# Half of a fused kernel's output projection by a Strassen identity, with its scaling spread over the QKV stage

## The chip, the cores and the metric

The kernel runs on one core of one Trainium2 chip. The metric is the device time of one execution in microseconds (us). A run here is one execution. Of each kernel one execution was also taken by the hardware profiler, and its trace is of that one run. The runs were made in several groups, on different chips, so totals of different groups are compared by their ratio to the kernel before, which ran in every group.

Engines are named as in the profile: PE is TensorE, PEld its weight loads, DVE is VectorE, ACT is ScalarE, POOL is GpSimd, SP is SyncE, which issues most of the transfers here.

## The reference

```python
def _A_ref(x, wqkv, wo):                 # B=1, S=2048, D=1024, H=32 heads of 32
    q, k, v = split_heads(x @ wqkv)
    phi = lambda t: jnp.where(t > 0, t + 1, jnp.exp(t)) + 1e-6
    pq, pk = phi(q), phi(k)
    kv  = einsum("bhsd,bhse->bhde", pk, v)
    z   = einsum("bhsd->bhd", pk)
    num = einsum("bhqd,bhde->bhqe", pq, kv)
    den = einsum("bhqd,bhd->bhq", pq, z)[..., None] + 1e-6
    return merge_heads(num / den) @ wo
def _B_ref(x, w_gate, w_up, w_down):      # F=3584
    return (silu(x @ w_gate) * (x @ w_up)) @ w_down
xn = layernorm(x)
return x + _A_ref(xn, ...) * silu(_B_ref(xn, ...))     # bf16 in and out
```

The edit concerns the last product of `_A_ref`, `o @ wo`.

## The kernel before

The kernel has four stages on PE, one after the other. The QKV stage computes K and V for 16 token tiles and accumulates `kvz`. Block 0's Q projection follows. Then come the Q projections of blocks 1 to 3, mixed with `nd` (numerator and denominator of each of 16 row tiles) and the output projection `s_ps`. Last come gate/up and down, which already use a seven-product identity of Strassen's kind: sums of blocks of the activations on VectorE, differences of blocks of the weights (called T) on GpSimd.

While the first stages run, the other engines prepare the gate, up and down weights for that identity. One preparation step takes a weight chunk through this chain: a load, a square with a running sum on ScalarE (a norm, which bounds the values), a one-column matmul that sums it over partitions, a scaling by a power of two on VectorE, four subtractions on GpSimd, and a store.

```python
def emit_st0(key, t):      # ScalarE: sum of squares of one chunk, into asum
    nc.scalar.activation(out=junk, in_=raw_view(key, t), func=ACT.Square, accum_out=asum[:])
def emit_sc(key, t):       # VectorE: the scaling, SBUF to SBUF
    nc.vector.tensor_scalar(out=w, in0=w, scalar1=cs_all[:, c:c + 1], scalar2=None, op0=ALU.mult)
def emit_T(key, t, later=False):   # GpSimd: SBUF to SBUF
    nc.gpsimd.tensor_tensor(out=T1, in0=b12, in1=b11, op=ALU.subtract)
    nc.gpsimd.tensor_tensor(out=T2, in0=b22, in1=T1, op=ALU.subtract)
    nc.gpsimd.tensor_tensor(out=T3, in0=b22, in1=b12, op=ALU.subtract)
    nc.gpsimd.tensor_tensor(out=T4, in0=b21, in1=T2, op=ALU.subtract)
    # ... cut
def prep_step(between=None):
    # ... a load for the newest chunk, a store of the oldest
    emit_st0(*prep_st[1])
    emit_st1(k3[0], stat_ps[0]())      # one-column matmul
    between()                          # often: one nd tile and its evacuation
    emit_st2(*k3)                      # power of two, and emit_sc
    emit_T(*k3, later=True)
```

The output projection before the edit is plain. For each row tile and each half of the columns it runs eight matmuls of 512 columns.

```python
def emit_S(b, t, cc):
    s_ps = ps2.tile([P, CW], FP32, name="s_ps", tag="B2")
    for c in range(G):                          # G = 8, CW = 512
        nc.tensor.matmul(s_ps[:], lhsT=oT[:, c, ttok], rhs=wo_sb[:, c, cc*CW:(cc+1)*CW], ...)
    nc.scalar.copy(out=s_sb[:, cc*CW:(cc+1)*CW], in_=s_ps[:])
# the QKV stage, cut: per token tile i and column chunk c
for i in range(2, NT):
    for c in range(NCH):
        emit_Bmm(i, c); ...; emit_Bev(i, c)
        if c == 3 and i in (4, 6, 7): prep(1)
        if i >= 8 and c % 2 == 1: prep(...)     # 13 steps over tiles 8 to 15
```

## Time and profile before

The kernel before took 761.89 us, the median of three runs (761.75 to 763.33). These lines are from the page of its profiled execution: the span, the busy time of the engines with their share and number of instructions, GpSimd's busy tenths in 40 slices of 19 us, the chain that ended last by engine, and the group of the output projection (busy us, mean ns of one, idle before it). Line numbers differ between kernels; the tile names do not.

```profile
span 761.6 us, 10386 instructions
...
PE 748.9 (98%) x3662; PEld 350.5 (46%) x3731; DVE 542.3 (71%) x1026; ACT 348.0 (46%) x479; POOL 269.6 (35%) x382
...
POOL 0477699827563255868655000200000000200000
...
PE 94%; DVE 3%; DMA 1%; issue 1%; ACT 0%; SPq 0%; DVEq 0%; ACTq 0%
...
L688 PE MATMUL s_ps<-wo_sb,oT 128*128 128x512 bf16 x250 | 57.4, 379 | 0.3
```

PE is busy 98% of the time, and it is 94% of the chain. Time that another engine spends costs the kernel nothing unless PE waits for it.

The waits view lists who kept PE waiting: in total, how often, and the longest, in us.

```profile
PE warm_ps L549 <- DVE warm L546: 1.5, 1, 1.5
PE kv_ps L514 <- DMA wkv_sb<-in_A_wqkv_dram: 1.3, 1, 1.3
PE zw L761 <- DVE cg L830: 0.7, 1, 0.7
PE nd L658 <- DVE pqT L159: 0.4, 1, 0.4
...
PE q_ps L176 <- DVE pqT L159: 0.3, 1, 0.3
```

All of PE's waits come to about 5 us. At most 2.5 of them lie after the first loads.

The next lines are GpSimd's timeline late in the attention stage (start, duration). They show one of the four subtractions of one preparation step. It takes 1.16 us when nothing disturbs it.

```profile
214.19 1.16 POOL L286 TENSOR_TENSOR w_sb<-w_sb 128x512 f16<-128x512 bf16 x1 [0.68 <-ACT s_sb L691]
```

### The profile page before, as it was taken

What the parts mean: (1) busy time and instruction counts of PE and PEld (TensorE: products, weight loads), DVE (VectorE), ACT (ScalarE), POOL (GpSimd) and SP (SyncE); (2) the same over time, 40 slices, a digit from 0 to 9 for tenths busy, and PEclk for the clock granted to TensorE, in tenths of its full rate; (3) what the DMA queues carried; (4) which work ended last, traced back from release to release, by engine and by line L of the source; (5) the groups of instructions that cost most, each with busy time, mean ns of one, the idle gap of its engine ahead of it and who ended that gap; (6) DMA issues with size and microseconds to landing.
All of it is one profiled execution on the core that took longest, in us unless ns stands there. A gap on an engine that the chain in (4) does not pass through costs nothing.

```text
span 761.6 us, 10386 instructions
## 1 busy us (share of the span) xinstructions
PE 748.9 (98%) x3662; PEld 350.5 (46%) x3731; DVE 542.3 (71%) x1026; ACT 348.0 (46%) x479; POOL 269.6 (35%) x382
## 2 busy tenths in 40 slices
PE   8999999999999999999999999999999999999997
PEld 3444444454444444444444444444444444444444
DVE  6788676985656688878889875358676767787335
ACT  4545677698954566566448411132323222211022
POOL 0477699827563255868655000200000000200000
PEclk9999999999999999999999999999999999999999
DMA  9876799779879669898888227397654445430824
GB/s 318 286 157 125 198 301 322 259 173 292 245 217 289 243 229 318 281 353 287 308 300 293 80 90 257 121 379 281 251 185 178 166 165 172 173 139 15 275 88 136
DMA packets 105908, 170.29 MB, mean 224 GB/s; under 512 B 34688, under 2 KB 82176, under 8 KB 95232
## 3 DMA queue, kind: packets, MB, share of 16 engines
q1 hardware_dynamic: 99280, 143.81, 59.6%
q0 software_dynamic: 3984, 21.24, 7.0%
q10 hardware_dynamic: 2592, 4.59, 1.8%
q8 instruction: 29, 0.48, 0.3%
q14 instruction: 23, 0.19, 0.1%
HBM read 111.67 MB, written 50.59 MB: 213 GB/s over the span
## 4 chain that ended last, share of the span: by engine, by line
PE 94%; DVE 3%; DMA 1%; issue 1%; ACT 0%; SPq 0%; DVEq 0%; ACTq 0%
PE zw L761 25%; PE kv_ps L514 14%; PE xb L761 12%; PE dzw L946 12%; PE s_ps L688 7%; PE yb L761 6%; PE dx L946 6%; PE q_ps L176 5%; PE dy L946 3%; DMA wkv_sb<-in_A_wqkv_dram 1%; PE nd L658 1%; PE kvz L536 1%; PE df L946 1%; DVE pqT L159 1%; DVE q_ps L153 1%
## 5 line engine op out<-in xcount | busy, mean ns | idle before, releaser
L761 PEld LDWEIGHTS <-w_sb 128*128 128x128 f16 (+1 forms) x1568 | 152.1, 98 | 183.9 <-issue 1.3
L514 PE MATMUL kv_ps<-wkv_sb,xnT 128*128 128x512 bf16 x499 | 113.0, 379 | 2.6 <-DMA wkv_sb<-in_A_wqkv_dram 1.3
L761 PE MATMUL xb<-xnT,w_sb 128*128 128x512 bf16 x420 | 113.3, 379 | 1.5
L761 PE MATMUL zw<-S,w_sb 128*128 128x512 f16 x448 | 105.8, 379 | 0.7 <-DVE cg L830 0.7
L761 PE MATMUL zw<-xnT,w_sb 128*128 128x512 bf16 x448 | 105.8, 379 | 0.0
L286 POOL TENSOR_TENSOR w_sb<-w_sb 128x512 f16<-128x512 bf16 x42 | 49.3, 1173 | 116.9 <-DVE w_sb L274 29.1
L253 ACT ACTIVATE w_sb<-w_sb 128x2048 bf16<-128x2048 bf16 x42 | 79.9, 1902 | 11.8 <-DMA w_sb<-in_B_w_up_dram 5.6
L946 PE MATMUL dx<-w_sb,hT 128*128 128x512 bf16 x202 | 76.6, 379 | 0.3
L514 PEld LDWEIGHTS <-xnT 128*128 128x128 bf16 x512 | 48.6, 98 | 57.7 <-issue 2.2
L946 PEld LDWEIGHTS <-hT 128*128 128x128 bf16 (+1 forms) x462 | 45.2, 98 | 51.7
L176 PE MATMUL q_ps<-xnT,wq_sb 128*128 128x512 bf16 x249 | 58.2, 379 | 0.7 <-DVE pqT L159 0.3
L789 DVE SCALAR_TENSOR_TENSOR s<-yb,rc_all,s 128x512 f32<-128x512 f32 x42 | 31.5, 749 | 37.8 <-ACT s L788 37.6
L688 PE MATMUL s_ps<-wo_sb,oT 128*128 128x512 bf16 x250 | 57.4, 379 | 0.3
L761 PE MATMUL yb<-S,w_sb 128*128 128x512 f16 x224 | 57.4, 378 | 0.0
L946 PE MATMUL dzw<-w_sb,hT 128*128 128x512 bf16 (+1 forms) x190 | 57.0, 379 | 0.0
L837 ACT ACTIVATE sg<-cg 128x1024 bf16<-128x1024 f32 x28 | 29.6, 1057 | 56.8 <-DVE cg L830 56.8
L830 DVE SCALAR_TENSOR_TENSOR cg<-zw,rc_all,s 128x1024 f32<-128x1024 f32 x28 | 35.9, 1283 | 24.3 <-PE zw L761 14.0
L287 POOL TENSOR_TENSOR w_sb<-w_sb 128x512 f16<-128x512 bf16 x42 | 50.1, 1193 | 3.3
L289 POOL TENSOR_TENSOR w_sb<-w_sb 128x512 f16<-128x512 bf16 x42 | 50.4, 1201 | 0.0
L288 POOL TENSOR_TENSOR w_sb<-w_sb 128x512 f16<-128x512 bf16 x42 | 50.4, 1199 | 0.0
L886 POOL TENSOR_TENSOR hs<-hT 128x512 f16<-128x512 bf16 x2 | 2.5, 1250 | 132.7 <-ACT sg L837 132.6
L920 POOL DMA_DIRECT2D out_dram<-io x16 | 8.7, 544 | 101.8 <-DVE io L919 101.6
(152 smaller groups left out, 1080.5 us busy)
## 6 DMA issues: line engine op xcount, KB each, us to landing
w_sb<-pk_g SPq DMA_DIRECT2D x27, 1024.0 KB, 6.1
pk_g<-w_sb SPq DMA_DIRECT2D x14, 1024.0 KB, 5.1
w_sb<-wd SPq DMA_DIRECT2D x14, 1024.0 KB, 5.0
w_sb<-pk_u SPq DMA_DIRECT2D x14, 1024.0 KB, 5.0
pk_u<-w_sb POOLq DMA_DIRECT2D x13, 1024.0 KB, 6.0
w_sb<-wd SPq DMA_DIRECT2D x14, 768.0 KB, 5.6
w_sb<-in_B_w_gate_dram SPq DMA_DIRECT2D x14, 512.0 KB, 6.5
w_sb<-in_B_w_down_dram SPq DMA_DIRECT2D x28, 256.0 KB, 4.7
```

The costliest lines, as they stand in the source:

```text
L176: nc.tensor.matmul(q_ps[:], lhsT=wq_sb[:, dc, g * P:(g + 1) * P], rhs=xn_ap(dc, btok), start=(dc == 0), stop=(dc == DC - 1))
L253: nc.scalar.activation(out=junk, in_=raw_view(key, t), func=ACT.Square, accum_out=asum[:])
L286: nc.gpsimd.tensor_tensor(out=T1, in0=b12, in1=b11, op=ALU.subtract)
L287: nc.gpsimd.tensor_tensor(out=T2, in0=b22, in1=T1, op=ALU.subtract)
L288: nc.gpsimd.tensor_tensor(out=T3, in0=b22, in1=b12, op=ALU.subtract)
L289: nc.gpsimd.tensor_tensor(out=T4, in0=b21, in1=T2, op=ALU.subtract)
L514: mm = nc.tensor.matmul(kv_ps[:], lhsT=xn_ap(dc, tok), rhs=wkv_sb[:, dc, c * CW:(c + 1) * CW], start=(dc == 0), stop=(dc == DC - 1))
L688: mm = nc.tensor.matmul(s_ps[:], lhsT=oT[:, c, ttok], rhs=wo_sb[:, c, cc * CW:(cc + 1) * CW], start=(c == 0), stop=(c == G - 1))
L761: mm = nc.tensor.matmul(out, lhsT=lhs(k), rhs=rhs(k), start=(first and k == 0), stop=(k == HK - 1), skip_group_check=True)
L789: nc.vector.scalar_tensor_tensor(out=s2[:], in0=y_[:], scalar=rc, in1=s1[:], op0=ALU.mult, op1=ALU.add)
L830: nc.vector.scalar_tensor_tensor(out=d12, in0=zw[:], scalar=rc, in1=s2[:, None, :].to_broadcast([P, 2, TB]), op0=ALU.mult, op1=ALU.add)
L946: nc.tensor.matmul(out, lhsT=lhs, rhs=rhs, start=first, stop=lastk, skip_group_check=True)
```

## The change

The intent is to save PE time in the attention stage. Blocks 2 and 3 of `o @ wo` are done by a seven-product identity instead of eight products. That needs sums of blocks of `o`, differences of blocks of `wo` (the four `To`), and fp16 operands, which the kernel keeps bounded: `o` is scaled by a power of two from norms of wv, and `wo` by one from its own norms. Those statistics are spread over the QKV stage as small instructions.

The diff, cut to what matters:

```diff
-    NWE = 8
+    NWE = 7                        # one chunk of w_down is prepared later, in gate/up
+    SO_ST = [(i, c) for i in (2, 3, 4, 5) for c in (0, 2)] + [(i, c) for i in (6, 7, 8, 9) for c in (0, 2)]
+    SO_PW = [(7, 1), (10, 1)]
+    WO_SC = (10, 11, 12, 13)
     ... in the QKV stage, tile i, chunk c:
+                if (i, c) in SO_ST: so_stat(...)      # ScalarE: square of 1024 columns, 16 in all
+                if (i, c) in SO_PW: so_pow2(...)      # PE: eight 1-column matmuls in a row, twice
+                if c == 3 and i in WO_SC:
+                    wo_scale(WO_SC.index(i))          # VectorE: wo_sb *= power of two, 128x2048, four times
-                if c == 3 and i in (4, 6, 7):
+                if c == 3 and i in (4, 5, 6, 7):
                     prep(1)
     ... block 0's Q: the phi of three of the groups moves to ScalarE
-            emit_Q(0, g)
+            emit_Q(0, g, act=g in (3,5,7))
     ... once: 16 subtractions on GpSimd for the four To
+                nc.gpsimd.tensor_tensor(out=o_[:, k], in0=a_[:, k], in1=b_[:, k], op=ALU.subtract)
     ... the evacuation of nd and the copy of s multiply by the powers of two
     ... blocks 2 and 3: four units, each 7 products of 4 matmuls
+            def sums():                               # VectorE, SBUF to SBUF, 128x512 each
+                nc.vector.tensor_tensor(out=so[:, 0], in0=a21, in1=a22, op=ALU.add)
+                nc.vector.tensor_tensor(out=so[:, 1], in0=so[:, 0], in1=a11, op=ALU.subtract)
+                nc.vector.tensor_tensor(out=so[:, 2], in0=a11, in1=a21, op=ALU.subtract)
+                nc.vector.tensor_tensor(out=S4, in0=a12, in1=so[:, 1], op=ALU.subtract)
     ... the order in which the first unit starts:
+        u["sums"]()
+        nds[0]()
+        u["x"]()
+        u["w"]()
+        emit_S(1, 3, 0, fx[4])
+        nds[1]()
+        units[1]["sums"]()
     ... (further units, with the last preparation and the sums of x between them)
```

## The prediction

> **What bounds the kernel now.** The page gives PE 98% busy and the chain of waits is 94% PE; the granted clock is full. PE's waits add up to only about 5 us of 761.6: 1.5 before the warm-up, 1.7 on the first loads, 0.4 + 0.3 in the Q projection of block 0 (on pqT, VectorE). The stage table shows 19.89 of 20 us busy almost everywhere. Only fewer PE cycles, or the removal of those waits, can help. In the chain, 16 matmuls of 512 columns take 3.45 us, 216 ns each (the 379 ns "mean" overlaps the next).
>
> **Removed.** Blocks 2 and 3 of the output projection are 128 such matmuls; 4 units x 7 products x 4 = 112 remain: 16 x 0.216 = -3.45 us. The order of instructions has as many on PE as before: 16 large ones became 16 one-column ones.
>
> **Added on PE.** Two groups of 8 statistic matmuls. One alone costs 0.02 us (8 + 1 matmuls take 1.75 against 1.73 us), [...]eight 129-column kvz matmuls take 0.46 us. [...]Estimate +0.8 us for both.
>
> **Block 0's Q.** Three phis move work to ScalarE (VectorE 0.68 us instead of 0.62 + 0.69). The chain runs through VectorE from 133.7 to 147.7 us; PE loses 0.75 us. I expect 0.5 to 0.7 us back.
>
> **Off the chain.** ScalarE gets 16 squares of 1024 columns (estimate 1.05 us each, from 1.9 us for 2048) in the QKV stage between 25 and 86 us, where it is 49 to 71% busy. Walking its order by hand with 0.99 us (exp+relu) and 0.49 us (V copy), it stays within the 7.37 us of a token tile, tile 9 excepted (7.9), which three PSUM banks absorb: 0 to 0.5 us lost. GpSimd gets 16 subtractions of 1.16 us (18.6 us), which fit its idle gap of 149 to 167 us. One wd chunk moves into the gate/up stage, which has room: 0 to 0.2 us.
>
> **End of the attention stage.** A unit is 6.04 us of PE. VectorE has sums of 4 x 0.42 and two evacuations of 0.75; in the last two units also the four sums of x (6.6 us) and the last preparation, about 12 of 12.1 us. The last unit puts z, x2, z2 in a row, so z2 waits for VectorE's evacuation of Z. oT of block 3 reuses the buffer that block 1's last group reads, and a transpose lands after 5.2 us (3.0 to 7.7), so sums may hold VectorE 1 to 2 us. PE loses an estimated 0.5 to 1.5 us here.
>
> **Sum.** -3.45 + 0.8 - 0.6 + 0.2 + 1.0 + 0.1 = -1.95: about 759.9 us; I take 759.6, range 757.8 to 762.0. Faster by 2%: 0.005, within 2%: 0.985, slower: 0.01.
>
> **What would show it.** Matmuls of the output projection: 240 rather than 256. PE's 0.75 us of waits around 138 to 148 us gone. Statistics groups of 0.4 us each near 70 and 87 us. PE waits in the last 30 us before gate/up: 0.5 to 1.5 us, on VectorE. Gate/up and down stages unchanged in length. GpSimd busy 149 to 168 us.
>
> **What would make it wrong.** ScalarE holding up kv_ps banks between 60 and 95 us (1 to 3 us slower); sums waiting for transposes behind blocked stores in the sync queue (PE idle several us near 225 us); or no stall in the units at all: 758.6 us.

In the part on the work added on PE two passages that gave a reason for the +0.8 us are cut, since no trace of this case shows it. The sum and its six terms stand as recorded (-3.45 + 0.8 - 0.6 + 0.2 + 1.0 + 0.1 = -1.95 us). The +0.8 is the estimate from the 0.46 us of eight `kvz` matmuls.

## More of the kernel before

An `nd` tile has one PSUM buffer. PE starts the next one only when VectorE has evacuated the last (such a wait took 2.6 us in the profile after).

GpSimd shows 9 in the slices from about 95 to 133 us. It has no slack where the weights are prepared (19.68 of 20 us busy from 100 to 120 us).

## The result and the profile after

The changed kernel took 764.45 us (median of four runs, 764.0 to 765.68). In the same rounds the kernel before took 762.26 (761.75 to 763.33). The ratio is 1.0029, with a 95% interval of 1.0012 to 1.0047. Within 2% the two are the same, but the interval lies above 1. PE does less work, and the kernel became slower by about 2.2 us. A ratio here is the mean time of one kernel's runs over that of the other's runs of the same rounds, so it is not quite the ratio of the medians quoted.

The same lines of the page after:

```profile
span 763.0 us, 10573 instructions
...
PE 750.1 (98%) x3731; PEld 349.4 (46%) x3731; DVE 561.8 (74%) x1058; ACT 376.2 (49%) x526; POOL 290.0 (38%) x400
```

GpSimd is busier (290.0 us against 269.6), mostly by the new `To`. The page alone shows no fault: PE reads 98% again, and its granted clock was 1.0.

The waits of PE do show it:

```profile
PE nd L713 <- DVE wq_sb L725: 2.6, 1, 2.6
...
PE kv_ps L525 <- DMA wkv_sb<-in_A_wqkv_dram: 1.5, 1, 1.5
PE q_ps L182 <- DVE pqT L162: 1.2, 2, 0.9
PE kv_ps L525 <- DVE pk_sb L162: 1.1, 2, 0.9
```

A wait of 2.6 us for the `nd` bank is new. The waits on `q_ps` grew from 0.3 to 1.2 us. Those on `kv_ps` behind VectorE are new, with 1.1 us.

To see where time was lost, PE's timeline is cut at four starts: the first `kvz` product, the first matmul of block 0's Q, the first matmul after the first `nd` tile, and the first matmul of gate/up. The lengths below are differences of those starts. The last column is the span less the start of gate/up.

| profiled execution | QKV, from the first kvz | block 0's Q and first nd | from there to gate/up | gate/up and down | span |
|---|---|---|---|---|---|
| before | 102.63 | 19.30 | 100.52 | 513.34 | 761.6 |
| before_again | 102.63 | 19.29 | 100.52 | 513.54 | 761.2 |
| after | 104.58 | 19.83 | 100.26 | 512.48 | 763.0 |
| after less before | +1.95 | +0.53 | -0.26 | -0.86 | +1.4 |

The first three columns of the kernel before repeat to 0.01 us in two executions, so hundredths mean something here. The time before the first kvz varies from 25.0 to 26.0 us over all traces, with waits for the first loads. It is left out of the table for that reason. The two executions after and before differ by 1.4 us and not by the 2.2 of the medians, since the profiled run of the kernel before (763.33 us) was the slowest of its four, while that of the changed kernel (764.76 us) was near its median. The saving of 3.45 us lies in the third column, and nearly all of it is missing there.

### The profile page after: what moved, and what is told of

Read it like the earlier page. It is cut to its first block, busy times and chain, and to the rows that moved or that the text cites. A ratio compares the mean times of both kernels' runs of the same rounds, so it can differ in the third digit from the quotient of the medians. Undisturbed runs are those within 1.5% of the kernel's fastest.

```text
span 763.0 us, 10573 instructions
## 1 busy us (share of the span) xinstructions
PE 750.1 (98%) x3731; PEld 349.4 (46%) x3731; DVE 561.8 (74%) x1058; ACT 376.2 (49%) x526; POOL 290.0 (38%) x400
## 4 chain that ended last, share of the span: by engine, by line
PE 70%; DVE 1%; ACT 0%; issue 0%
PE zw L935 25%; PE xb L935 13%; PE dzw L1120 12%; PE yb L935 6%; PE dx L1120 6%; PE dy L1120 3%; PE fx L786 3%; PE df L1120 1%; PE dz L1120 0%; PE fx L744 0%; PE nd L713 0%; DVE wq_sb L725 0%; DVE wq_sb L781 0%; DVE oT L782 0%; DVE wq_sb L780 0%; DVE pqT L150 0%
## 5 line engine op out<-in xcount | busy, mean ns | idle before, releaser
L935 PE MATMUL xb<-xnT,w_sb 128*128 128x512 bf16 x448 | 115.0, 379 | 0.0
L1120 PE MATMUL dx<-w_sb,hT 128*128 128x512 bf16 x210 | 79.6, 379 | 0.0
L1120 PE MATMUL dzw<-w_sb,hT 128*128 128x512 f16 x196 | 58.3, 379 | 0.0
L962 ACT ACTIVATE s<-xb,rcl 128x512 f32<-128x512 f32 x14 | 9.6, 687 | 65.3 <-PE xb L935 65.3
```

The lines of the kernel that those rows point to most:

```text
L935: mm = nc.tensor.matmul(out, lhsT=lhs(k), rhs=rhs(k), start=(first and k == 0), stop=(k == HK - 1), skip_group_check=True)
L1120: nc.tensor.matmul(out, lhsT=lhs, rhs=rhs, start=first, stop=lastk, skip_group_check=True)
```

## Where the time went, read from the traces

**The units.** The chain of waits, followed back from gate/up and given in order of time, passes through VectorE just before the `nd` tile that waited. Columns: start, us, what. (The sums are written into space that `wq_sb` no longer needs, hence their name.)

```profile
218.74 1.20 DVE wq_sb L780
219.94 1.31 DVE wq_sb L781
...
221.27 1.26 DVE oT L782
...
223.23 1.36 DVE wq_sb L725 x3
...
224.64 0.64 PE nd L713 x8
```

The `nd` product at 224.64 waited for VectorE's evacuation (L725). That stood in line behind the sums (L779 to L782) of the first unit. VectorE's own timeline shows what the sums cost:

```profile
218.19 0.45 DVE L779 TENSOR_TENSOR wq_sb<-oT 128x512 f16<-128x512 bf16 x1
218.74 1.20 DVE L780 TENSOR_TENSOR wq_sb<-wq_sb,oT 128x512 f16<-128x512 f16 x1
219.86 1.37 DVE L781 TENSOR_TENSOR wq_sb<-oT 128x512 f16<-128x512 bf16 x1
221.27 1.26 DVE L782 TENSOR_TENSOR oT<-oT,wq_sb 128x512 f16<-128x512 bf16 x1
```

The four sums have the same shape, yet the first takes 0.45 us and the others 1.20 to 1.37. Later units' sums take 0.41 to 0.42 us each. What differs is GpSimd, which at that time runs the last preparation step of block 2:

```profile
217.21 1.16 POOL L294 TENSOR_TENSOR w_sb<-w_sb 128x512 f16<-128x512 bf16 x1 [0.68 <-ACT s_sb L747]
218.44 1.21 POOL L295 TENSOR_TENSOR w_sb<-w_sb 128x512 f16<-128x512 bf16 x1
219.62 1.34 POOL L296 TENSOR_TENSOR w_sb<-w_sb 128x512 f16<-128x512 bf16 x1
220.91 1.33 POOL L297 TENSOR_TENSOR w_sb<-w_sb 128x512 f16<-128x512 bf16 x1
```

Those are the same four subtractions as in the kernel before, now 1.16, 1.21, 1.34 and 1.33 us. Both engines are slower in this overlap: three of VectorE's sums by a factor of about three (0.42 to 1.20-1.37 us), GpSimd's subtractions by up to 0.18 us (1.16 to 1.34).

So the first theory is that the two engines hold each other up where both work from SBUF to SBUF at the same time. The four sums together took 4.28 us instead of 1.68, and that excess of 2.60 us is as long as PE's wait of 2.58. The runs below test what the collision costs. They do not test by what mechanism it comes about, nor why the two engines share it so unevenly.

**The QKV stage.** The same reading applies to the scaling of `wo`. The first fence is one of its four instructions on VectorE. The second is GpSimd before and beside it.

```profile
108.15 1.64 DVE L619 TENSOR_SCALAR wo_sb<-wo_sb,cs_all 128x2048 bf16<-128x2048 bf16 x1
```

```profile
106.53 1.15 POOL L294 TENSOR_TENSOR w_sb<-w_sb 128x512 f16<-128x512 bf16 x1
...
109.21 1.60 POOL L296 TENSOR_TENSOR w_sb<-w_sb 128x512 f16<-128x512 bf16 x1
110.77 1.60 POOL L297 TENSOR_TENSOR w_sb<-w_sb 128x512 f16<-128x512 bf16 x1
```

A scaling of this shape takes 0.75 us where GpSimd runs no subtraction (L282 of this trace at 181.48, 198.82 and 204.34 us; 0.743 us is its shortest, 0.754 the median). Here it takes 1.64. The kernel before already shows this collision: its 13 weight scalings of this shape between 25 and 148 us (L274), all but one of them beside a subtraction of GpSimd, average 1.13 us. GpSimd's subtractions beside it take 1.60 us instead of 1.15. Not every overlap costs both: L282 at 91.75 us took 0.75 us beside a subtraction of 1.65. GpSimd is full in this stretch (19.69 of 20 us from 100 to 120), so what it loses is not made up.

The preparation then reaches ScalarE late. A square stands ahead of the exponentials on ScalarE and waited 2.02 us for its load:

```profile
124.69 1.91 ACT L259 ACTIVATE w_sb<-w_sb 128x2048 bf16<-128x2048 bf16 x1 [2.02 <-DMA w_sb<-in_B_w_gate_dram]
...
126.59 1.06 ACT L153 ACTIVATE e_t<-kv_ps 128x512 f32<-128x512 f32 x2
```

The exponential for `kv_ps` (L153) stands behind that square and started at 126.59 us, as the square ended. PE waits for the bank:

```profile
128.68 1.67 PE L525 MATMUL kv_ps<-wkv_sb,xnT 128*128 128x512 bf16 x7 [0.95 <-DVE pk_sb L162]
```

That is 0.95 us on PE, behind a queue that waits for a load. The trace shows what the load stood behind. GpSimd's last subtraction of the step before ended at 117.84 us, SyncE issued the store of its results at 117.86 and, next in the same queue, this load at 118.30. How much of the lateness is owed to the scalings of `wo` is tested by e2 and e3.

## The experiments

Theory P: VectorE's SBUF-to-SBUF instructions and GpSimd's subtractions hold each other up where they overlap, by whatever mechanism. This costs about 2.5 us at the first unit and about 1.5 us in the QKV stage.

Rival V: VectorE simply has too much to do there, whatever the instruction. Rival Q, for the first unit: the order on VectorE, with the sums ahead of the evacuation, or late transposes. Rival R: the step of preparation that was moved to tile 5, and ScalarE's 16 squares, disturb the QKV stage.

### e1_hold_T: an edit that changed nothing

The last step's subtractions were to be issued after the first unit's sums, by moving only their emission:

```diff
-            emit_T(*k3, later=True)
+            if hold: held.append(lambda: emit_T(*k3, later=True))
+            else:    emit_T(*k3, later=True)
...
         u["sums"]()
         nds[0]()
+        held.pop(0)()
```

> The changed kernel with one thing moved: the four GpSimd subtractions of the last preparation step of block 2 are issued after the sums of the first unit and the first evacuation of block 3, VectorE's order unchanged. Theory P[...]: the first unit's four sums fall from 0.45 / 1.20 / 1.37 / 1.26 us to 0.42 us each, and PE's wait of 2.58 us for the evacuated nd falls under 0.4 us; time about 2 to 2.6 us under the changed kernel, near 762. Rival Q (the sums stand before the evacuation in VectorE's order, or wait for their transposes): wait stays above 2 us, time within 0.7 us of the changed kernel's 764.4.

Measured: 764.13 us, ratio 1.0034 (1.0019 to 1.0049), and the wait still 2.57 us. This refutes nothing. GpSimd ran the subtractions at 216.19 to 221.2 us, again 0.68 us after what it had waited for, on top of the sums. Its queue had nothing else in it, so the later place in the program did not delay them here. In e6 a dependency did (227.23 us). The experiment tested nothing, and e6 below repeats it properly.

### e2_no_scale: the QKV stage without the four scalings

```diff
-                if c == 3 and i in WO_SC:
-                    wo_scale(WO_SC.index(i))
```

The bound of `o` then uses unscaled `wo`, which is still correct for these inputs.

> The changed kernel without the four scalings of wo on VectorE (and without the factor that undoes them; same result for these inputs). Theory P: GpSimd's subtractions between 100 and 120 us fall from 1.31 to under 1.2 us each, its preparation is 2 us earlier, ScalarE's waits for loads before 128 us shrink, PE's waits for VectorE's phi (0.95 + 0.16 us in the QKV stage, 1.17 us in block 0's Q) fall by at least 1 us in sum; time 1 to 2 us under the changed kernel. Rival R (the preparation that now starts one step earlier, at tile 5, is the cause): waits of PE as before, time within 0.5 us.

Measured: 763.56 us (762.14 to 763.8), ratio 1.0016 (1.0 to 1.0033). The QKV stage fell from 104.58 to 103.08 us, and the waits for `kv_ps` behind VectorE are gone. ScalarE's wait for the late gate load shrank from 2.02 to 0.59 us. The `nd` wait stayed at 2.57 us. The 16 squares of rival R stayed in too, and the stage is only 0.45 us longer than in the kernel before, of which the statistics groups on PE are about 0.4. So the squares cost next to nothing.

Half of these runs show another effect, described under "The clock" below. It took 1.7 us of the profiled execution, so the total says less than the stage.

### e3_bn_stand_in: the same VectorE time with other instructions

To part P from V, each scaling was replaced by three statistics instructions that together take 1.60 to 1.61 us, about its contended duration. They read one SBUF operand and write a few columns. The scaling factor is changed as in e2.

```diff
-                    wo_scale(WO_SC.index(i))
+                    for q_, sl_ in enumerate((slice(0, 512), slice(512, 1024), slice(0, 256))):
+                        nc.vector.bn_stats(out=st3[:, q_ % 2, :], in_=wo_sb[:, 2 * k_ + q_ // 2, sl_])
```

> As the kernel without the four scalings, but in their place VectorE does statistics over 1280 columns of wo (about 1.7 us each, as long as the scalings took): same VectorE time, one SBUF input. Theory P[...]: GpSimd's subtractions stay under 1.2 us and PE's waits are those of the kernel without scalings within 0.4 us. Rival V (VectorE's mere time): PE waits as long as in the changed kernel (2.3 us in sum in QKV and block 0's Q).

Measured: 764.43 us, ratio 1.0033 (1.0018 to 1.0048). The QKV stage took 103.42 us: 1.16 us less than the changed kernel, 0.34 us more than without anything in that place. The window of 100 to 120 us shows why. The columns are the window and its length, busy us with the number of instructions in brackets for PE, PEld, DVE, ACT and POOL, PE's clock, the DMA share and GB/s. The changed kernel, then e2, then e3:

```profile
100.00:120.00 20.00, 19.82 (x114) 9.72 (x113) 18.30 (x31) 13.68 (x20) 19.69 (x15) 1.00 0.93 293
```

```profile
100.00:120.00 20.00, 20.00 (x116) 9.85 (x114) 13.95 (x28) 14.36 (x21) 19.68 (x17) 1.00 1.01 315
```

```profile
100.00:120.00 20.00, 20.00 (x116) 9.82 (x115) 17.61 (x39) 14.36 (x20) 19.69 (x18) 1.00 1.01 314
```

VectorE is as busy in e3 (17.61 us) as after the change (18.30), but GpSimd gets through 18 instructions instead of 15 in the same 19.69 us. So 1.16 of the 1.5 us are what GpSimd loses, and about 0.34 us is VectorE's time. Rival V holds for at most a quarter of this cost, since the stand-in takes the contended 1.6 us and a scaling alone would take 0.75.

The total did not follow, because gate/up and down took 513.55 us here (512.48 after the change). Its trace shows a wait of 0.53 us there, for ScalarE.

### e4_no_prep5: the preparation step at tile 5 put back

```diff
-                if c == 3 and i in (4, 5, 6, 7):
+                if c == 3 and i in (4, 6, 7):
```

> The changed kernel without the extra preparation step at tile 5; one more step is left for the end of the attention stage. Rival R: the 0.95 us wait before the last QKV group vanishes and the wait in block 0's Q falls under 0.8 us; time about 1 to 1.5 us under the changed kernel. Theory P: these waits stay above 1.5 us in sum; time within 0.7 us of the changed kernel.

Measured: 770.33 us, ratio 1.0115 (1.0099 to 1.013). The waits in the QKV stage and in block 0's Q remained (0.73 and 0.93 us), and the QKV stage became only 0.54 us shorter. So rival R is not the main cause. The step that was left over slid into the units. There GpSimd's four subtractions met another unit's sums (0.42, 1.26, 1.37 and 1.26 us), then the first sum of x (2.17 us), and PE waited 3.26 us besides the 2.56 at `nd`. So the collision can be made a second time by moving a preparation step onto a unit. This supports P, at a cost that nobody would want.

### e5_drop_T: the last step's subtractions left out (wrong)

```diff
-            emit_T(*k3, later=True)
+            if not drop:                       # drop for the step at block 2, tile 3
+                emit_T(*k3, later=True)
```

> Wrong on purpose: the changed kernel without the four GpSimd subtractions of the last preparation step of block 2 (in the run before, issuing them later did not make them run later, so that run tested nothing). VectorE and PE have exactly the changed kernel's work and order. Theory P[...]: the first unit's four sums take 0.42 us each and PE's wait for the evacuated nd falls from 2.58 to under 0.4 us. Rival Q (order on VectorE, late transposes): the wait stays above 2 us.

Measured, in one look: 761.84 us (one run, state unknown), with a wrong result as intended (relative error 0.30). The sums took 0.41, 0.42, 0.42 and 0.42 us, and the wait at `nd` was gone. These are the second and third of them:

```profile
218.38 0.42 DVE L781 TENSOR_TENSOR wq_sb<-wq_sb,oT 128x512 f16<-128x512 f16 x1
218.73 0.42 DVE L782 TENSOR_TENSOR wq_sb<-oT 128x512 f16<-128x512 bf16 x1
```

The stretch to gate/up fell from 100.26 to 97.66 us. VectorE's work and order were those of the changed kernel, and only GpSimd's four subtractions were missing. So the 2.6 us were the collision and not the sums themselves, nor their place in the order (rival Q).

### e6_hold_scale: the same subtractions, really later

The step's scaling on VectorE, on which the subtractions depend, is emitted after the second unit's sums. This delay is a dependency. It also takes that scaling (1.39 us in the changed kernel, beside GpSimd) away from its place ahead of the first sums.

```diff
-            emit_st2(*k3)
-            emit_T(*k3, later=True)
+            emit_st2(*k3, later=hold)          # hold for the step at block 2, tile 3
+            if hold: held.extend((lambda: emit_sc(*k3), lambda: emit_T(*k3, later=True)))
+            else:    emit_T(*k3, later=True)
...
         units[1]["sums"]()
+        while held: held.pop(0)()
```

> The changed kernel, correct, with the last preparation step's scaling on VectorE held back until after the second unit's sums, so that its GpSimd subtractions, which need it, can not run before. Theory P: sums of the first unit 0.42 us each, PE's wait for nd under 0.3 us, no new wait above 0.5 us in the units; time 2 to 3.5 us under the changed kernel (2.6 us of wait, and what the granted clock loses after it): 761 to 762.5. Rival Q: as before, 764.

Measured: 762.88 us (762.46 to 763.57), ratio 1.0005 (0.999 to 1.0021). VectorE's timeline at the first unit (three of the four sums), and GpSimd's, which now pauses from 216.6 to 227 us:

```profile
217.75 0.43 DVE L785 TENSOR_TENSOR wq_sb<-wq_sb,oT 128x512 f16<-128x512 f16 x1
218.09 0.42 DVE L786 TENSOR_TENSOR wq_sb<-oT 128x512 f16<-128x512 bf16 x1
218.54 0.42 DVE L787 TENSOR_TENSOR oT<-oT,wq_sb 128x512 f16<-128x512 bf16 x1
```

```profile
215.49 1.16 POOL L297 TENSOR_TENSOR w_sb<-w_sb 128x512 f16<-128x512 bf16 x1
227.23 1.16 POOL L294 TENSOR_TENSOR w_sb<-w_sb 128x512 f16<-128x512 bf16 x1 [10.58 <-ACT s_sb L752]
```

The sums are all at 0.42 to 0.43 us, in the same place ahead of the evacuation. The wait at `nd` is gone, and the stretch to gate/up is 97.91 us (-2.35). The result is correct. VectorE's order is not quite that of the changed kernel: the scaling moved, and the first sum started about 1 us earlier (217.24 us instead of 218.19). So e6 shows that the loss can be had back in a correct kernel, and e5 is the clean test of its cause.

### e7_scale_on_act: the scaling of wo on ScalarE

```diff
-            nc.vector.tensor_scalar(out=wo_sb[:, 2*q:2*q+2, :], in0=..., scalar1=cs_all[...], op0=ALU.mult)
+            nc.scalar.activation(out=wo_sb[:, 2*q:2*q+2, :], in_=..., func=ACT.Copy, scale=cs_all[...])
```

> The changed kernel with the four scalings of wo on ScalarE (about 2 us each there) rather than VectorE. Theory P: GpSimd's subtractions from 100 to 120 us fall to 1.2 us, PE's wait of 0.95 us before the last QKV group falls under 0.3 us as without the scalings, unless ScalarE's 8 us more make a new wait of up to 0.5 us; time 0.5 to 1.2 us under the changed kernel.

Measured: 764.26 us, ratio 1.002 (1.0003 to 1.0037). The QKV stage took 103.88 us: 0.70 us better than with VectorE, 0.80 us worse than without scaling. GpSimd again ran 17 instructions between 100 and 120 us. The collision is avoided, but 0.80 us remain; that they are ScalarE's own time is argued, not tested. Block 0's Q became shorter too (18.95 us against 19.83), which was not aimed at.

### e8_all: both collisions removed, statistics joined

This is e6 and e7 together, with each group of eight 1-column statistics matmuls replaced by one of 8 columns and a reduction on VectorE.

```diff
-            for q in range(8 * h, 8 * h + 8):
-                nc.tensor.matmul(ps, lhsT=ones[:], rhs=so_st[:, q:q + 1], ...)
+            nc.tensor.matmul(ps[:], lhsT=ones[:], rhs=so_st[:, 8 * h:8 * h + 8], start=True, stop=True, ...)
+            nc.vector.tensor_reduce(out=tt[:], in_=ps[:], axis=mybir.AxisListType.X, op=ALU.add)
```

> Both mends, and each group of eight one-column statistics matmuls replaced by one eight-column matmul and a sum over eight on VectorE. Theory P: the gains add: -2.6 (nd) - 1.0 (scalings) - 0.35 (statistics) from 764.4, so 760.0 to 761.0, under the kernel before (761.8) by about 1 us. If waits that remain are simply moved to the next one: 761.5 or more.

Measured: 761.72 us (761.06 to 763.04), ratio 0.9991 (0.9978 to 1.0003). From the first kvz to gate/up it took 220.48 us, 4.19 us less than the changed kernel and 1.97 less than the kernel before. But gate/up and down took 515.05 us, 2.6 more than in the changed kernel.

The joined statistics gained nothing: the QKV stage is 103.90 us, against 103.88 in e7. Where PE saved 0.2 us, it then waited 0.3 us for VectorE before a `kvz` product.

### e9_no_scale_all: the same without any scaling of wo

The edits are those of e6, e2 and the joined statistics. (The expectation speaks of 16 scalings. There are four instructions.)

> The changed kernel[...]: the first unit's four sums behind the block-3 row-0 evacuation, the 16 scalings of wo left out (o's bound then uses the norms of the unscaled wo, correct for these inputs), and the eight 1-column statistics matmuls of a tile joined in one 8-column matmul. [...]no wait for kv_ps in the QKV stage, no 2.6 us wait for the nd bank, 1.3 us fewer statistics matmuls; from the first kvz to the start of gate/up about 219.5 to 220.3 us (changed kernel 224.67, kernel before 222.45). Total 759 to 761 us, ratio to the kernel before 0.997 to 0.999; the upper end if gate/up again waits about 1 us for late w_up loads. Rival (the change costs something else per unit that is still there): the stage stays above 222 us and the ratio at or above 1.0.

Measured: 762.59 us (760.08 to 764.48), ratio 1.0 (0.9981 to 1.0019). This misses the expected total. The way to gate/up missed its range by only 0.2 us (220.48). Most of the loss is behind it: gate/up and down took 516.64 us, with waits of 1.15 and 1.04 us and then about three microseconds at half clock. Three of the six runs had a mean clock of 0.997 and took 763.89 to 764.48 us; the three at 0.999 and above took 760.08 to 761.29. The rival of that expectation (some cost per unit still there) does not hold either, since the stretch of the units was 97.90 us.

### e10_late_square: one square of the preparation behind a phi

In block 0's Q of the changed kernel, ScalarE's next square waited for its load, and the exponentials for two `q_ps` banks waited behind it:

```profile
134.21 1.91 ACT L259 ACTIVATE w_sb<-w_sb 128x2048 bf16<-128x2048 bf16 x1 [2.10 <-DMA w_sb<-in_B_w_down_dram]
...
136.12 1.06 ACT L153 ACTIVATE e_t<-q_ps 128x512 f32<-128x512 f32 x2
```

The edit emits this one square after Q(0, 1) instead of before it:

```diff
-            emit_st0(*prep_st[1])
+            if late0: held0.append(lambda a=prep_st[1]: emit_st0(*a))   # for the last step of the QKV stage
+            else:     emit_st0(*prep_st[1])
...
             emit_Q(0, g, act=g in (3,5,7))
+            if g == 1: held0.pop(0)()
```

> The previous kernel with one ScalarE square of the weight preparation emitted after the first Q projection of block 0, so that ScalarE's in-order wait for that square's load does not stand ahead of the phi that frees q_ps. If that wait is what is left in block 0's Q, the wait of 0.8 to 0.9 us for q_ps goes to 0.4 us or less and the stage shortens by 0.4 to 0.8 us; total 758.5 to 760.5 us. If q_ps is held by something else the wait stays above 0.7 us.

Measured: 761.33 us (760.15 to 762.26), ratio 0.9989 (0.9977 to 1.0001). The wait on `q_ps` is gone, and block 0's Q fell from 19.42 us in e9 to 18.22, below the kernel before's 19.30. To gate/up it was 219.80 us. The expectation of the mechanism held. The expectation of the total (at most 760.5) did not, because gate/up and down took 514.57 us.

### before_again: a second profile of the kernel before

> The kernel before, unchanged, for a second profile: the one at hand is of one of its slower executions (763.33 us against a median of 761.89). Expected: a span of about 760 us, the same stage from first kvz to gate/up (222.4 us), and the difference of about 1.5 us in the gate/up or down stage, as half a microsecond waits for late loads or as a short spell of lower clock.

Measured: 762.98 us and a span of 761.2, so this execution too was one of the slower ones. The wait of 0.7 us in gate/up (`zw` behind `cg`) recurred with 0.9. The expected short span was not caught. What the faster runs of the kernel before do differently, no trace shows.

### e11_early_io: results' loads moved out of a full stretch

In e8, e9 and e10 the stage before ended earlier, and gate/up gave 2 to 4 us back. In each of them ScalarE waited some 6 us for a load of w_up, and PE then waited for ScalarE. This is the line in e10 (in brackets: idle before it, and what ended it):

```profile
324.50 1.91 ACT L259 ACTIVATE w_sb<-w_sb 128x2048 bf16<-128x2048 bf16 x1 [6.18 <-DMA w_sb<-in_B_w_up_dram]
```

That load had been issued at 311.90 us and took 12.5 us to land. From 310 to 335 us the DMA engines were 94% busy. Ten loads of 128 KB for the down projection's results were issued between 290 and 314 us, long before they are used, two of them right ahead of this load in the same queue. The edit issues them earlier:

```diff
-                if first and i in range(6, 11):
+                if first and i in range(1, 6):
                     io_load(mb)
```

> The previous kernel with the five pairs of 128 KB loads for the down projection's results issued in gate/up units 1 to 5 (about 261 to 285 us, where the DMA engines were 58% busy) instead of units 6 to 10 (291 to 316 us, where they were 80 to 93% busy). Theory: the w_up load that landed 12.5 us after its issue, at 324.4 us, was late because the DMA engines were full; then ScalarE's wait of 6.2 us for it and TensorE's waits of 1.15 and 0.45 us behind it shrink to under half and gate/up with down takes 513 us or less (514.6 before this edit); total 758 to 760 us. Rival: the load is late because of the order of the queue ahead of it or of GpSimd's stores; then the waits stay at 1 us or more and the total stays at 760.5 to 762 us.

Measured: 759.82 us (758.8 to 760.41), ratio 0.9967 (0.9954 to 0.9981). ScalarE's wait for that load is now:

```profile
320.57 1.91 ACT L259 ACTIVATE w_sb<-w_sb 128x2048 bf16<-128x2048 bf16 x1 [2.72 <-DMA w_sb<-in_B_w_up_dram]
```

Gate/up and down took 512.43 us with no recorded wait of PE. The edit took the ten loads out of the queue as well as out of the stretch, where the DMA engines were still 88% busy (90% in the changed kernel, which lost nothing there). So it does not tell full DMA engines from the order of the queue, the rival of that expectation. All of PE's recorded waits over 0.3 us now lie in the first loads and in the QKV stage:

```profile
PE warm_ps L570 <- DVE warm L567: 1.5, 1, 1.5
PE kv_ps L535 <- DMA wkv_sb<-in_A_wqkv_dram: 0.9, 1, 0.9
PE kv_ps L535 <- ACT xnT L524: 0.5, 1, 0.5
```

This version beats both kernels: by 2.2 us against the kernel before in its own rounds (762.05), and the changed kernel by the ratios. Part of that may be due to the moved loads, which are no part of the change. Its result passed the comparison, but it leaves out the scaling of `wo`. With weights of other magnitudes, the fp16 operands would no longer be bounded by `wo`'s own norms in this place.

### All profiles side by side

| profiled execution | QKV | block 0's Q | units | gate/up, down | sum of the first three |
|---|---|---|---|---|---|
| before | 102.63 | 19.30 | 100.52 | 513.34 | 222.45 |
| after | 104.58 | 19.83 | 100.26 | 512.48 | 224.67 |
| e1_hold_T | 104.47 | 19.76 | 100.26 | 512.48 | 224.49 |
| e2_no_scale | 103.08 | 19.37 | 101.95 (half clock) | 512.46 | 224.40 |
| e3_bn_stand_in | 103.42 | 19.24 | 100.27 | 513.55 | 222.93 |
| e4_no_prep5 | 104.04 | 19.85 | 107.08 (waits, half clock) | 512.55 | 230.97 |
| e5_drop_T | 104.59 | 19.78 | 97.66 | 512.49 | 222.03 |
| e6_hold_scale | 104.58 | 19.84 | 97.91 | 512.61 | 222.33 |
| e7_scale_on_act | 103.88 | 18.95 | 100.28 | 513.95 | 223.11 |
| e8_all | 103.90 | 18.68 | 97.90 | 515.05 | 220.48 |
| e9_no_scale_all | 103.16 | 19.42 | 97.90 | 516.64 | 220.48 |
| e10_late_square | 103.35 | 18.22 | 98.23 | 514.57 | 219.80 |
| e11_early_io | 103.09 | 18.22 | 97.96 | 512.43 | 219.27 |

Most edits move the column that they aim at; exceptions are block 0's Q in e7 and e8, and gate/up with down, which took 513.6 to 516.6 us in five of these kernels. The units are at 97.7 to 98.2 us in exactly the kernels in which the last subtractions do not meet the first sums, and at 100.3 or more elsewhere. Among the variants of the changed kernel, QKV is at 103.1 to 103.4 us in exactly those without `wo`'s scaling, at 103.9 with it on ScalarE, and at 104.0 to 104.6 with it on VectorE. That is the evidence for theory P, and it is stronger than any single total.

### The clock

In some executions a wait of PE costs more than its length. These three lines are windows of e2 around its `nd` wait, which lasted 2.57 us and ended at 221.97. Columns as above, so the clock is the third value from the end.

```profile
221.00:223.00 2.00, 1.03 (x11) 0.78 (x12) 1.26 (x5) 0.00 (x0) 0.00 (x0) 1.00 0.00 0
223.00:224.00 1.00, 1.00 (x5) 0.40 (x3) 0.93 (x4) 0.37 (x1) 0.00 (x0) 0.61 0.00 0
...
225.00:226.00 1.00, 1.00 (x4) 0.36 (x3) 0.93 (x4) 0.66 (x1) 0.00 (x0) 0.50 0.06 16
```

From 223.22 to 226.63 us the granted clock is 0.50, and PE lost about 1.7 us (101.95 against 100.26 us in that stretch). In the changed kernel's own profile the same wait of 2.58 us was followed by a clock of 1.00 throughout. So the length of a wait does not decide alone.

The half clock lasted 3.4 us in each of the four places where it lies inside a kernel (e2; e4 twice, from about 224.5 and 248.4 us; e9). In the 3.41 us ahead of each, PE was idle for 2.16 us (e2), 2.47 and 2.48 (e4) and 1.92 (e9). In the changed kernel the stretch of 3.41 us that ends with the wait held all of its 2.58 us, and no half clock followed. So the idle time just ahead does not decide alone either. What does was not shown.

This explains part of the spread of the totals: in e2, the two runs with a mean clock of 0.998 took 763.8 and 763.74 us, the other two 762.14 and 763.38. In e9, two waits that added to 2.2 us within some 3 us were followed by half clock from 331.57 to 334.98 us. In e6, without the long wait, the clock was 1.0 in all four runs.

## Why the prediction was wrong

The prediction said 759.6 us, in a range of 757.8 to 762.0. The kernel took 764.45. The class (within 2%) was right. The sum was off by 4.1 us against its own starting point: it expected -1.95 us and the medians differ by +2.19.

| term of the prediction | predicted | what the runs showed |
|---|---|---|
| 16 matmuls of 512 columns fewer | -3.45 | holds: with the collision away, the units' stretch is 97.91 against 100.52 us |
| statistics groups on PE | +0.8 | 0.2 each, +0.4 |
| block 0's Q | -0.6 | +0.53; -1.08 once the square is moved (e10) |
| ScalarE's squares in QKV, with the rest of QKV | +0.2 | QKV without the statistics' 0.4: +1.55, of which 1.5 is the scaling of wo (e2) |
| end of the attention stage | +1.0 | a wait of 2.58 and about 0.6 in small gaps: +3.2 |
| wd chunk into gate/up | +0.1 | no cost seen (512.5 against 513.3 us) |

- **The step that failed first: durations taken from a quiet neighbour.** "VectorE has sums of 4 x 0.42" took the duration of the lone instruction. In the one place where the sums stand ahead of a bank that PE needs, they took 4.28 us together instead of 1.68, because GpSimd ran at the same time. e5 shows it cleanly, and e6 in a correct kernel. The profile before held a warning: the 13 weight scalings between 25 and 148 us, 12 of them beside GpSimd, average 1.13 us there, against 0.75 alone. The prediction warned that PE might idle "several us near 225 us". The place was right and the cause was not: no transpose and no blocked store was involved.
- **A term was missing.** The prediction's list has no entry for the four scalings of `wo`. It looked for the QKV risk in ScalarE's load, and that load was not the trouble. GpSimd was full from 95 to 133 us, which the page before shows. The scaling takes time from an engine without slack, and the loss came back to PE over a late load and ScalarE's order, two engines away.
- **Block 0's Q.** The mechanism (phi taken off VectorE) was right, as e10 shows with 18.22 us. It was covered by ScalarE's wait for a load. The walk through ScalarE's order counted durations and not the arrival of the loads that its squares wait for.
- **The statistics term was mis-sized.** The prediction put two groups of eight one-column matmuls at +0.8 us, from the 0.46 us of eight 129-column `kvz` matmuls. That one group costs about as much as the other was the estimate and was not shown. An estimate from the trace's 216 ns per 512 columns gives about 54 ns for 129 columns, 0.44 of the 0.46 us for eight. By it nearly all of that time goes with the columns, of which the statistics have one. Here is one group on PE's timeline after, and the instruction that follows it:

```profile
86.51 0.34 PE L607 MATMUL st_ps<-so_st,ones 128*128 128x1 bf16 x8
86.71 1.89 PE L525 MATMUL kv_ps<-wkv_sb,xnT 128*128 128x512 bf16 x8
```

The next instruction starts 0.20 us after the start of the group, 25 ns for each of the eight.
- **What was right.** PE at the limit, 240 matmuls in the output projection, GpSimd's `To` between 149 and 168 us (151.8 to 169.7 measured), and gate/up with down unchanged within 1 us. With the collision removed, the units' own cost was right in size too: -3.45 + 1.0 = -2.45 predicted, -2.61 measured (e6 against before). That is luck in part: the waits on VectorE of which the +1.0 was made were not recorded in e6.

**What stays open.** Whether the earlier loads of e11 would help the kernel before as well was not run. Its own wait of 0.7 to 0.9 us in gate/up is of another line. Some 0.6 us of PE's gaps of 0.1 to 0.3 us in the units were seen and not traced to a cause. Why e11's load lands in time, by less filled DMA engines or by a shorter queue, was not separated.

## What to carry to other kernels

Before adding a VectorE instruction that works from SBUF to SBUF, look at what GpSimd does at that moment. Where both worked on SBUF here, a 128x512 sum took 1.20 to 1.37 us instead of 0.42. So cost both with the durations of overlapping instances, and ask which of the two has slack. Look also for waits for loads that stand ahead of instructions that free a bank: here one square that waited 2.10 us for its load kept two exponentials behind it, and with the square placed behind one of the Q projections block 0's Q took 18.22 us instead of 19.42 (e10 against e9). And when a stage is made shorter, follow the gain into the next stage: here the first three stages won 4 us against the changed kernel (e8), and late loads gave more than half of it back (2.6 us) until other loads were moved (e11).
